# Block-sparse attention with the sampled blocks gathered on chip and the MLP woven in by half sequences

## The chip, the cores and the metric

The kernel runs on one core of one Trainium2 chip. The metric is the device time of one execution in microseconds (us), so smaller is better. A comparison is repeated in rounds on one chip, the kernel before next to the changed one.

Engines are called PE (TensorE, matrix products), PEld (its weight loads), ACT (ScalarE), DVE (VectorE), POOL (GpSimd) and SP (SyncE, here an issuer of DMAs). The traces list the instructions of each apart, as its queue; what the order of such a queue can cost is measured below for DVE (9.6 and 23.1 us of waiting in front of two copies).

## The reference, cut to what matters

```python
batch, n_heads, seq, head_dim = 4, 8, 768, 64
block, n_blocks, n_rand = 32, 24, 3
scores = (q @ k.T) / sqrt(64)
mask = |blk_i - blk_j| <= 1  or  blk_i in (0, 23)  or  blk_j in (0, 23)
for qb in range(24):
    for kb in sampled_blocks[qb]:        # 3 random key blocks, known only at run time
        mask[qb's rows, kb's columns] = True
x = softmax(where(mask, scores, -1e9)) @ v      # reshaped to 3072 x 512
out = gelu(x @ w_in) @ w_out                    # w_in 512 x 2048, w_out 2048 x 512
```

A query block in the middle sees its own key block and two neighbours, the first and the last block, and three sampled ones, so at most 8 blocks of 24. The first and the last query block see all 24. The inputs are float32, the kernels compute in bf16. q and k are drawn at 0.1 times a normal deviate, so all scores are close to zero.

## The kernel before: the parts that the change and the argument touch

```python
# attention, two heads at a time; all 24 x 24 blocks are computed, masked ones too.
# The mask is added inside the product: 64 extra rows of q (one-hot) and k (mask row).
for gi, (b, h) in enumerate(grp):
    for t in range(NT):                                   # 6 tiles of 128 keys
        sp = spsum_pool.tile([P, S], F32, tag="sp")
        for c0 in range(0, S, 512): nc.tensor.matmul(sp[:, c0:c1], ...)
        ex = exps_pool.tile([P, S], BF16, tag="ex")
        nc.scalar.activation(ex, sp, AF.Exp, scale=scale)          # L168: 128 x 768
# ... 6 x 6 products with V for each head, division, and then:
        nc.sync.dma_start(out=x_dram[...], in_=ao)                 # x goes to DRAM, 192 DMAs

# only after all attention: weights, and x back from DRAM, transposed
nc.gpsimd.dma_start(out=w_in_sb, in_=...); nc.gpsimd.dma_start(out=w_out_sb, in_=...)
for ki in range(KIN):
    nc.sync.dma_start(out=xT[:, ki, :], in_=x_dram[:, ki*P:(ki+1)*P], transpose=True)
# ... MLP in 6 tiles of 512 tokens: matmul hp (L214), Gelu (L218), matmul op (L220)
```

The softmax here doesn't subtract the row's maximum and nothing guards it: scores larger than these inputs give would overflow.

## Time and profile before

The kernel before took 463.65 us (median of 4 runs, 461.46 to 466.43) in the measurement beside the change.

| stretch, us | what happens | PE busy |
|---|---|---|
| 0 to 23 | set-up, mask | 0.42 |
| 23 to 243 | attention, no MLP | 179.5 of 220 |
| 243 to 292 | hole: weights and x are fetched | 4.88 of 49 |
| 292 to 467 | MLP, no attention | 166.04 of 175 |

The table comes from the windows view of the kernel before (a profiled execution with a span of 467.0 us). Its columns are: window and length in us, then busy us (and count of instructions) of PE, PEld, DVE, ACT and POOL, the granted PE clock as a fraction of full speed, the busy share of the DMA engines, GB/s.

```profile
0.00:23.00 23.00, 0.42 (x3) 0.26 (x4) 2.40 (x16) 1.28 (x1) 7.56 (x23) 1.00 0.37 32
23.00:145.00 122.00, 99.62 (x1038) 61.60 (x1037) 70.04 (x429) 78.19 (x104) 49.23 (x75) 0.94 1.12 94
145.00:243.00 98.00, 79.85 (x887) 49.60 (x883) 55.03 (x339) 66.07 (x89) 28.72 (x46) 0.93 0.84 73
243.00:292.00 49.00, 4.88 (x11) 1.46 (x12) 0.00 (x0) 0.96 (x1) 1.90 (x2) 0.51 1.13 150
292.00:467.00 175.00, 166.04 (x741) 66.64 (x756) 0.00 (x0) 69.78 (x121) 0.00 (x0) 0.99 0.10 37
```

The reader should see three stages with different limits. In the fourth line PE all but stands still (4.88 us busy of 49) and its granted clock is 0.51 on average, against 0.93 in the line before and 0.99 in the one after.

The groups view of the kernel before names the two costs that the change aims at. After the bar stand busy us and mean ns of one, then the idle time of the engine just before these instructions and what ended it.

```profile
L168 ACT ACTIVATE ex<-sp 128x768 bf16<-128x768 f32 x192 | 144.3, 808 | 92.0 <-PE op L176 56.7
L214 PE MATMUL hp<-xT,w_in_sb 128*128 128x512 bf16 x375 | 96.1, 384 | 45.8 <-DMA w_in_sb<-in_moe_w_in_dram 29.4
```

And the DMA view of the same kernel shows why the hole is there (the last number is us from issue to landing):

```profile
w_in_sb<-in_moe_w_in_dram POOLq DMA_DIRECT2D x1, 2048.0 KB, 26.2
w_out_sb<-in_moe_w_out_dram POOLq DMA_DIRECT2D x1, 2048.0 KB, 38.8
xT<-x_dram SPq DMA_TRANSPOSE x4, 28.4
```

The 192 dense exps fill 144 us of ACT, and the first MLP products wait 29.4 us for weights that are asked for only when the attention is over.

### The profile page before, as it was taken

Reading aid. Unit: us, or ns where it says so; the run is one execution under the profiler, and the core shown is the slowest. Engines: PE = TensorE matmul, PEld = TensorE weight load, DVE = VectorE, ACT = ScalarE, POOL = GpSimd, SP = SyncE. Lnnn points to the kernel's source line nnn. Section 1 sums busy time; section 2 is a strip of 40 time slices with the busy share of each in tenths; the row PEclk is TensorE's granted clock in tenths of the full one; section 3 lists DMA queues with packets and bytes.
Section 4 is the critical chain, followed back from the end, with each engine's and each line's share of the span. In section 5 each row is a group of like instructions: output and inputs, shape, how many; then the busy total and the mean of one; then the engine's idle time right before and its main releaser. Section 6 shows DMA issues by size and latency. Waiting matters only on the chain.

```text
span 467.0 us, 7913 instructions
## 1 busy us (share of the span) xinstructions
PE 350.8 (75%) x2672; PEld 179.6 (38%) x2688; DVE 127.5 (27%) x783; ACT 216.3 (46%) x314; POOL 87.4 (19%) x145
## 2 busy tenths in 40 slices
PE   0087878787788788889740003999999999999994
PEld 0054545554455455555420001333433443443341
DVE  1055756554556465566430000000000000000000
ACT  1055767667567676777720000335344353433533
POOL 1453434324334333441000000000000000000000
PEclk9999999888999898899975555999999999999999
DMA  0799999799899799997219999002011020200202
GB/s 1 68 133 99 96 101 98 70 91 84 73 100 97 70 98 96 100 80 60 27 22 156 131 176 162 1 0 91 0 41 51 0 91 0 84 7 0 92 0 90
DMA packets 174200, 33.11 MB, mean 71 GB/s; under 512 B 168528, under 2 KB 170576, under 8 KB 174160
## 3 DMA queue, kind: packets, MB, share of 16 engines
q0 software_dynamic: 77856, 13.64, 38.1%
q1 hardware_dynamic: 96304, 18.98, 25.8%
q8 instruction: 21, 0.34, 0.3%
q14 instruction: 19, 0.16, 0.1%
HBM read 27.34 MB, written 9.44 MB: 79 GB/s over the span
## 4 chain that ended last, share of the span: by engine, by line
PE 54%; DMA 15%; ACT 12%; SPq 9%; issue 5%; DVE 3%; POOL 0%; DVEq 0%; ACTq 0%; POOLq 0%
PE op L220 18%; PE hp L214 17%; ACT ex L168 11%; PE sp L165 10%; DMA x_dram<-ao 9%; SPq L198 9%; PE op L176 6%; DMA sb_i_80<-in_sampled_blocks_dram 2%; PE pt L151 1%; DMA xT<-x_dram 1%; DVE ao L182 1%; DMA q_sb<-in_q_dram 1%; DMA k_sb<-in_k_dram 1%; DVE kT L155 1%; DVE recip L180 1%
## 5 line engine op out<-in xcount | busy, mean ns | idle before, releaser
L168 ACT ACTIVATE ex<-sp 128x768 bf16<-128x768 f32 x192 | 144.3, 808 | 92.0 <-PE op L176 56.7
L214 PE MATMUL hp<-xT,w_in_sb 128*128 128x512 bf16 x375 | 96.1, 384 | 45.8 <-DMA w_in_sb<-in_moe_w_in_dram 29.4
L165 PE MATMUL sp<-qT,kT 128*128 128x512 bf16 (+1 forms) x384 | 103.9, 352 | 8.8 <-ACT ex L168 3.2
L218 ACT ACTIVATE g<-hp 128x512 bf16<-128x512 f32 x96 | 57.1, 597 | 98.8 <-PE hp L214 98.3
L220 PE MATMUL op<-w_out_sb,g 128*128 128x512 bf16 x377 | 94.9, 380 | 3.2 <-ACT g L218 2.5
L176 PE MATMUL op<-v_sb,ex 128*128 128x65 bf16 x1152 | 80.2, 199 | 22.6 <-DVE ao L182 13.0
L176 PEld LDWEIGHTS <-ex 128*128 128x128 bf16 x1152 | 62.6, 101 | 66.5 <-DVE ao L182 27.1
L214 PEld LDWEIGHTS <-w_in_sb 128*128 128x128 bf16 x384 | 37.8, 99 | 93.5 <-issue 50.7
L151 PE MATMUL pt<-identity,q_sb 128*128 128x128 bf16 x192 | 44.1, 230 | 26.3 <-DMA q_sb<-onehot_sb 21.7
L182 DVE TENSOR_SCALAR ao<-op,recip 128x64 bf16<-128x64 f32 x192 | 49.4, 279 | 22.5 <-DMA x_dram<-ao 21.9
L152 DVE COPY qT<-pt 128x128 bf16<-128x128 bf16 x192 | 41.3, 215 | 45.4 <-PE sp L165 23.8
L220 PEld LDWEIGHTS <-g 128*128 128x128 bf16 x384 | 30.3, 97 | 58.1 <-ACT g L218 33.8
L165 PEld LDWEIGHTS <-kT 128*128 128x128 bf16 x384 | 34.7, 103 | 18.3 <-issue 15.6
L180 DVE RECIPROCAL recip<-op 128x1 f32<-128x1 f32 x192 | 28.8, 164 | 25.8 <-PE op L176 17.1
L151 PEld LDWEIGHTS <-q_sb 128*128 128x128 bf16 x192 | 19.6, 102 | 34.8 <-issue 27.6
L133 POOL DMA_DIRECT2D q_sb<-in_q_dram x32 | 26.7, 834 | 20.7 <-DVE maskrow_sb L100 5.6
L140 POOL DMA_DIRECT2D v_sb<-in_v_dram x32 | 26.5, 828 | 6.6 <-POOL v_sb L139 6.5
L135 POOL DMA_DIRECT2D k_sb<-in_k_dram x32 | 27.0, 843 | 0.6 <-PE pt_822 L154 0.5
L218 ACT ACT_TABLE_LOAD x1 | 1.3, 1283 | 52.7 <-PE hp L214 52.7
L139 POOL MEMSET v_sb<- 128x6 bf16 x32 | 4.1, 129 | 102.2 <-PE pt L151 86.3
L154 PEld LDWEIGHTS <-k_sb 128*128 128x128 bf16 x192 | 19.5, 102 | 9.8 <-issue 7.6
L225 ACT COPY os<-op 128x512 f32<-128x512 f32 x24 | 12.9, 596 | 3.1 <-DMA out_dram<-os 2.6
(413 smaller groups left out, 94.0 us busy)
## 6 DMA issues: line engine op xcount, KB each, us to landing
out_dram<-os SPq DMA_DIRECT2D x24, 256.0 KB, 2.1
q_sb<-onehot_sb SPq DMA_DIRECT2D x32, 96.0 KB, 3.1
q_sb<-in_q_dram POOLq DMA_DIRECT2D x32, 96.0 KB, 3.8
k_sb<-maskrow_sb SPq DMA_DIRECT2D x32, 96.0 KB, 4.0
k_sb<-in_k_dram POOLq DMA_DIRECT2D x32, 96.0 KB, 4.1
v_sb<-in_v_dram POOLq DMA_DIRECT2D x32, 96.0 KB, 3.7
x_dram<-ao SPq DMA_DIRECT2D x192, 16.0 KB, 2.0
w_in_sb<-in_moe_w_in_dram POOLq DMA_DIRECT2D x1, 2048.0 KB, 26.2
```

The source lines that it names most:

```text
L135: nc.gpsimd.dma_start(out=k_sb[:, :, :D], in_=k[b, h].rearrange("(t p) d -> p t d", p=P))
L151: nc.tensor.transpose(pt, q_sbs[gi][:, t, :], identity)
L152: nc.vector.tensor_copy(qT[:, t * P:(t + 1) * P], pt)
L165: nc.tensor.matmul(sp[:, c0:c1], lhsT=kTs[gi][:, t * P:(t + 1) * P], rhs=qTs[gi][:, c0:c1], start=True, stop=True)
L168: nc.scalar.activation(ex, sp, AF.Exp, scale=scale)
L176: nc.tensor.matmul(op, lhsT=exps[gi][t][:, m * P:(m + 1) * P], rhs=v1_sbs[gi][:, t, :], start=(t == 0), stop=(t == NT - 1))
L180: nc.vector.reciprocal(recip, op[:, D:D + 1])
L182: nc.vector.tensor_scalar_mul(ao, op[:, 0:D], recip)
L198: nc.sync.dma_start(out=xT[:, ki, :], in_=x_dram[:, ki * P:(ki + 1) * P], transpose=True)
L214: nc.tensor.matmul(hp, lhsT=w_in_sb[:, ki, m * P:(m + 1) * P], rhs=xT[:, ki, n * NTILE:(n + 1) * NTILE], start=(ki == 0), stop=(ki == KIN ...
L218: nc.scalar.activation(g, hp, AF.Gelu)
L220: nc.tensor.matmul(op_tiles[ti], lhsT=g[:, ti * P:(ti + 1) * P], rhs=w_out_sb[:, m, :], start=(m == 0), stop=(m == KOUT - 1))
```

## The change

The intent is fourfold. Only the visible blocks are computed. The sampled blocks are gathered at run time: K inside SBUF by an indirect copy on POOL, V from a scratch tensor in DRAM by an indirect DMA, which POOL also issues. x stays on chip. And the MLP of one half sequence (384 tokens) is woven together with the attention of the next: the hidden layer of half h with the preparation of the next batch, the output layer of half h with the attention of half h+1. The weights load early.

```diff
-    mask24_dram = dram.tile([NB, NB], F32)
-    x_dram = dram.tile([N_TOK, D_MODEL], BF16)
... (dense attention, DMA transposes and separate MLP removed)
+    def prep_v(b, v_st, st):
+        pj = v_pj[0]
+        nc.vector.tensor_copy(
+            pj[:, :, :, 0:D], v_st.rearrange("p h (j d) -> p j h d", d=D))
... (to DRAM, and back in natural order)
+    def gather_v(b, hb, st):
...
+        for i in range(NQH):                                   # 11 query blocks of a half
+            qi = hb * NQH + i
+            nc.gpsimd.indirect_dma_start(
+                out=vg[:, i, :], out_offset=None, in_=v_dram[b][:, :],
+                in_offset=bass.IndirectOffsetOnAxis(ap=idx_v[:, qi:qi + 1], axis=0))
...
+    def gather_k(b, hb, hp, st):                               # one of 4 head pairs
...
+        nc.gpsimd.indirect_copy(dv[:, 0:32, :], kv, idx_k[:, hb, 0:2], i_know_this_is_slow=True)
+        nc.gpsimd.indirect_copy(dv[:, 32:44, :], kv, idx_k[:, hb, 2:3], i_know_this_is_slow=True)
...
+    for half in range(2 * B):
...
+            if hb == 0:
+                for w in "kqv":
+                    load(b + 1, w)                             # issued by POOL (casts to bf16)
+                vst = stage["v"]
+                fill.append(lambda nst=nst, b=b, vst=vst: prep_v(b + 1, vst, nst))
+            for hp in (2 * hb, 2 * hb + 1):
... (transposes of K and Q of the next batch)
+                fill.append(lambda hp=hp, nst=nst, b=b: gather_k(b + 1, 0, hp, nst))
+            if hb == 1:
+                fill.append(lambda nst=nst, b=b: gather_v(b + 1, 0, nst))
+        merge(hidden_steps(b, hb, st), fill)
+
+        if half + 1 < 2 * B:
+            merge(attention_steps(nb_, nhb, sts[nb_]), output_steps(b, hb, st))
+            if nhb == 0:
+                for hp in range(NPAIR):
+                    gather_k(nb_, 1, hp, sts[nb_])
+                gather_v(nb_, 1, sts[nb_])
```

A static scheduler moves instructions within each engine's queue before anything runs.

## The prediction

> **What bounds the kernel now.** Busy time by stretch (the windows view) shows a sequence. 0-23 us: set-up, PE busy 0.4 us. 23-243 us: attention, with no MLP work; PE busy 82% (179 us of 220), ACT 66%. 243-292 us: a hole, PE busy 4.9 us, clock 0.51: the weights are loaded only now (26 us and 39 us from issue to landing) while the DMA transposes bring x back from DRAM (28 us median). 292-467 us: MLP, PE busy 166 of 175 us; the chain of waits is almost all matmuls, 8 in 1.73-1.79 us (0.22 us each for 512 columns).
>
> **Removed.** (a) The 49 us hole: weights load early, x stays on chip. (b) 192 DMA writes of x and 64 DMA fills of mask columns. (c) Dense scores: 192 exps of 128x768 at 808 ns, 144 us of ACT; 384 wide score matmuls (104 us PE busy) and 1152 PV matmuls. (d) The strict order attention then MLP.
>
> **Added, by estimate from durations in the trace.**
> PE: the MLP stays, 384 output matmuls x 0.22 plus 512 hidden ones of 384 columns x 0.165 = 169 us. Attention becomes about 1984 + 384 small matmuls; six 65-column matmuls with their loads now take 0.36 us including 0.2 us latency, so some 30 ns each: 74 us[...] and 304 transposes x 56 ns = 17 us. PE floor about 275 us.
> ACT: exps (1024+704+128 columns x 32, 768 x 16) about 78 us, Gelus 64 x 0.8 = 52 us, plus 16 table loads at 1.28 us, since Exp and Gelu now alternate by half. About 150 us; not the limit.
> DVE: PSUM copies[...], masks, normalisation: about 130 us.
> POOL: the new risk. 32 K gathers of 44 indices. [...]V: 88 indirect DMAs at 1.0-1.3 us (plain ones took 0.83 us), about 100 us. POOL total 270-330 us: about as long as PE.
>
> **Critical path.** Prologue: sampled blocks land at 10 us (as now), then index arithmetic on DVE, first K gather near 13-15 us; V goes through DRAM and back; the gathers of half 0 run serially on POOL before the w_in loads are issued. First MLP matmul about 50-60 us, with PE mostly idle. Then eight halves of hidden + (output merged with next attention): PE floor per half 21 us MLP + about 12-13 us attention, with stalls 36 us. 55 + 8 x 36 = 343 us.
>
> **Prediction.** 345 us, 8 in 10 between 300 and 415. Faster by over 2%: 0.93; within 2%: 0.03; slower: 0.04.
>
> **What would show each step.** No hole with PE idle and clock near 0.5 after the prologue; ACT exp time about halved; small matmuls issued some 30 ns apart; MLP about 170 us of PE; table loads about 16; POOL busy above 70% of the span; in the chain, PE first and POOL gathers second, the gathers above all in the prologue and in second halves of each batch, whose K and V gathers are queued only just before.
>
> **What would make it wrong.** K gathers over 9 us each: POOL alone then needs over 400 us and bounds the kernel. [...] Short PE waits lowering the clock. In the other direction, gathers of 2-3 us and a prologue of 35 us would give under 310 us.

What no trace of the kernel before supports is cut from this text, terms of sums among it. The PE terms that are left come to 260 us (169 + 74 + 17); the sum, 275 us, holds a cut allowance, and so do the 12 to 13 us of attention for a half (the terms left give 11.4 us). Of POOL's total of 270 to 330 us the V gathers are about 100 us; most of the rest stood for the K gathers, an estimate that no trace supported. As for the terms that are left: a single 65-column matmul was recorded at 199 ns on average (L176, x1152), which is the 0.2 us of latency, and the 0.165 us and 56 ns are estimates, the 0.22 us of 512 columns (8 in 1.79 us) scaled to 384 and 128. For the clock, the profile before shows 0.93 to 0.94 during the attention, where PE is busy for 82% of the time, and 0.99 in the MLP, where it is busy for 95%.

## The result, and the profile after

The changed kernel took 430.6 us (median of 4 runs, 427.82 to 431.70) against 463.65 us. The ratio is 0.927, with a 95% interval of 0.921 to 0.934. All ratios in this document are taken from the fast runs of the same rounds, so they are not quite the ratio of the medians quoted. The change is faster, as predicted, but the time is 86 us above the predicted 345 us and outside the range of 300 to 415 us.

The groups view after, to be held against the one of before:

```profile
L286 POOL INDIRECT_COPY kg<-tk,idx_k 128x1024 bf16 x32 | 56.4, 1763 | 112.5 <-issue 44.0
L441 ACT ACTIVATE g<-hp 128x768 bf16<-128x768 f32 x64 | 51.5, 811 | 170.6 <-PE hp L439 76.3
...
L287 POOL INDIRECT_COPY kg<-tk,idx_k 128x384 bf16 x32 | 36.9, 1154 | 14.6 <-issue 13.3
...
L256 POOL DMA_INDIRECT vg<-v_dram_189,idx_v x22 | 21.2, 963 | 12.9 <-PE og L354 6.7
```

The exps of 144 us are gone; ACT as a whole fell from 216.3 to 142.9 us (the page's list of busy times). A K gather is the pair of lines L286 and L287, a V gather is L256. But PE, with 288.6 us of work in a span of 429.1 us, is busy for only 67% of it. The windows view after, in slices of 20 us, shows where it stands still:

```profile
80.00:100.00 20.00, 4.80 (x60) 2.30 (x57) 1.31 (x3) 2.27 (x5) 14.52 (x15) 0.50 0.41 90
...
120.00:140.00 20.00, 10.97 (x82) 5.81 (x82) 4.03 (x8) 0.00 (x0) 14.77 (x15) 0.74 0.93 234
...
180.00:200.00 20.00, 3.77 (x82) 2.23 (x83) 0.00 (x0) 3.83 (x5) 13.46 (x12) 0.67 0.34 71
...
340.00:360.00 20.00, 19.24 (x267) 12.18 (x267) 8.04 (x16) 14.34 (x19) 8.72 (x6) 1.00 0.04 15
```

The last line is what the prediction had in mind (19.2 of 20 us). The first three are not. All the slices in which PE is busy for less than 12 of 20 us lie in the first 160 us or between 180 and 200 us, that is in the first half of the run. The starts of the hidden layers of the eight halves, read from the timeline of the hidden-layer matmuls, say the same: 64.3, 137.4, 212.9, 250.0, 299.5, 338.6, 374.7 and 404.3 us. The prologue is 64 us (55 predicted). The six halves from 212.9 us on take 216 us, the predicted 36 each on average. That agreement is chance: their starts lie 29.6 to 49.5 us apart, and on another chip the same six took 197.5 us (below). The first two take 73.1 and 75.5 us, together 77 us more than 2 x 36. So in this sum the whole miss sits in the prologue (9 us) and in these two halves (77 us).

The waits view after gives suspects (in all, how often, longest, in us):

```profile
ACT g L441 <- remote: 61.6, 6, 30.8
...
DVE v_pj L235 <- DMA st_v<-in_v_dram: 37.4, 3, 23.0
...
PE og L354 <- DMA vg<-v_dram_186,idx_v: 20.2, 17, 4.7
PE od L376 <- DVE xd L344: 20.1, 1, 20.1
```

L235 is the copy of a new batch's V on DVE. The timeline of DVE shows it at work (start, length, what; in brackets the idle time before it and what ended that):

```profile
118.82 0.73 DVE L264 COPY pm<-st_k 128x768 bf16<-128x768 bf16 x1
129.15 0.96 DVE L235 COPY v_pj<-st_v 128x3072 bf16<-128x3072 bf16 x1 [9.61 <-DMA st_v<-in_v_dram]
...
179.04 0.56 DVE L344 TENSOR_TENSOR x<-og,rc 128x384 bf16<-128x384 f32 x1
202.65 0.96 DVE L235 COPY v_pj<-st_v 128x3072 bf16<-128x3072 bf16 x1 [23.05 <-DMA st_v<-in_v_dram]
```

At 118.82 us DVE ends a copy. The next instruction in its queue is the copy of V for a later batch, whose data have only been asked for at 118.45 us. DVE waits 9.6 us, later 23.1 us, with ready work behind it: after 179.04 us the normalisation of finished attention (L343, L344) stood in the queue, and PE waited for that in turn (20.1 us, L376). DVE did not take that work past the waiting copy: it did nothing at all in the window from 180 to 200 us (0.00 us busy), and L343 and L344 follow at 203.52 and 203.71 us, behind the copy at 202.65 us. The scheduler had moved these copies ahead: among DVE's working instructions the two stand at places 118 and 148, while in the kernel that keeps them in program order (x1_prepv_pinned, below) they stand at 166 and 238.

The timeline of POOL shows why the load was not there:

```profile
72.76 1.65 POOL L286 INDIRECT_COPY kg<-tk,idx_k 128x1024 bf16 x1 [2.00 <-issue]
74.82 1.11 POOL L287 INDIRECT_COPY kg<-tk,idx_k 128x384 bf16 x1 [0.41 <-issue]
77.94 1.99 POOL L286 INDIRECT_COPY kg<-tk,idx_k 128x1024 bf16 x1 [2.00 <-issue]
80.74 1.11 POOL L287 INDIRECT_COPY kg<-tk,idx_k 128x384 bf16 x1 [0.82 <-issue]
82.03 1.06 POOL L256 DMA_INDIRECT vg<-v_dram_186,idx_v  x1 [0.18 <-issue]
83.39 0.99 POOL L256 DMA_INDIRECT vg<-v_dram_186,idx_v  x1 [0.30 <-issue]
...
94.76 0.96 POOL L256 DMA_INDIRECT vg<-v_dram_186,idx_v  x1 [0.30 <-issue]
95.72 0.97 POOL L89 DMA_DIRECT2D st_k<-in_k_dram  x1
96.67 0.93 POOL L89 DMA_DIRECT2D st_q<-in_q_dram  x1
97.56 0.92 POOL L89 DMA_DIRECT2D st_v<-in_v_dram  x1
```

Four K gathers, each a pair of instructions, then eleven V gathers, then, at 95.72 us, the issue of the loads for the next batch. POOL takes these one after the other from 20.9 us on. The loads cast float32 to bf16, and this kernel issues them all on POOL, so they queue behind gathers that have nothing to do with them. One K gather takes 5.18 us from start to start (72.76 to 77.94): 1.65 and 1.11 us recorded, and 2.00 and 0.41 us before them in which POOL waits for nothing that the profile shows. The 2.00 us belong to the gather: none of the 32 has less before it, and before the V gather that follows one at 82.03 us they are missing. One V gather takes 1.26 us from start to start. So the gathers of one half cost POOL 4 x 5.18 + 11 x 1.26 = 34.6 us, and of all eight 277 us.

### The profile page after: what moved, and what is told of

The parts are those of the page before. It is cut to its first block, busy times and chain, and to the rows that moved or that the text cites. A ratio compares the mean times of both kernels' runs of the same rounds, so it can differ in the third digit from the quotient of the medians.

```text
span 429.1 us, 8099 instructions
## 1 busy us (share of the span) xinstructions
PE 288.6 (67%) x3532; PEld 174.0 (41%) x3568; DVE 148.2 (35%) x327; ACT 142.9 (33%) x192; POOL 206.7 (48%) x212
## 5 line engine op out<-in xcount | busy, mean ns | idle before, releaser
L439 PE MATMUL hp<-xT,w_in_sb 128*128 128x384 bf16 x512 | 94.4, 341 | 27.9 <-ACT g L441 17.5
L286 POOL INDIRECT_COPY kg<-tk,idx_k 128x1024 bf16 x32 | 56.4, 1763 | 112.5 <-issue 44.0
L441 ACT ACTIVATE g<-hp 128x768 bf16<-128x768 f32 x64 | 51.5, 811 | 170.6 <-PE hp L439 76.3
L354 PEld LDWEIGHTS <-pt 128*32 128x32 bf16 (+1 forms) x992 | 28.7, 103 | 37.8 <-issue 24.3
L287 POOL INDIRECT_COPY kg<-tk,idx_k 128x384 bf16 x32 | 36.9, 1154 | 14.6 <-issue 13.3
L306 DVE TENSOR_TENSOR pt<-pt,mask_x 128x768 bf16<-128x768 bf16 x32 | 22.9, 723 | 61.0 <-ACT pt L305 58.6
L268 PE MATMUL ps<-ident,pm 128*128 128x128 bf16 x192 | 19.0, 256 | 24.6 <-DVE ident L110 15.9
L354 PE MATMUL og<-vg,pt 128*32 128x65 bf16 x704 | 18.9, 207 | 20.6 <-DMA vg<-v_dram_186,idx_v 20.2
L459 DVE COPY os<-op 128x512 f32<-128x512 f32 x24 | 16.6, 690 | 33.2 <-PE op L455 26.2
L256 POOL DMA_INDIRECT vg<-v_dram_189,idx_v x22 | 21.2, 963 | 12.9 <-PE og L354 6.7
L256 POOL DMA_INDIRECT vg<-v_dram_188,idx_v x22 | 21.4, 973 | 12.4 <-PE og L354 6.4
L256 POOL DMA_INDIRECT vg<-v_dram_187,idx_v x22 | 21.8, 989 | 7.4 <-issue 6.4
L376 PE MATMUL od<-v_nat,pd 128*64 128x65 bf16 x192 | 11.1, 215 | 20.1 <-DVE xd L344 20.1
L256 POOL DMA_INDIRECT vg<-v_dram_186,idx_v x22 | 21.3, 968 | 6.5 <-issue 6.5
L343 DVE RECIPROCAL rc<-og 128x6 f32<-128x6 f32 x32 | 6.1, 192 | 46.8 <-PE og L354 46.7
L376 PEld LDWEIGHTS <-pd 128*64 128x64 bf16 x192 | 9.1, 127 | 23.5 <-issue 22.6
```

The costliest lines, as they stand in the source:

```text
L256: nc.gpsimd.indirect_dma_start(out=vg[:, i, :], out_offset=None, in_=v_dram[b][:, :], in_offset=bass.IndirectOffsetOnAxis(ap=idx_v[:, qi:q ...
L268: nc.tensor.transpose(ps[:, j, :], pm[:, j, :, :].rearrange("p h d -> p (h d)"), ident)
L286: nc.gpsimd.indirect_copy(dv[:, 0:32, :], kv, idx_k[:, hb, 0:2], i_know_this_is_slow=True)
L287: nc.gpsimd.indirect_copy(dv[:, 32:44, :], kv, idx_k[:, hb, 2:3], i_know_this_is_slow=True)
L306: nc.vector.tensor_tensor(pt[:, 0, :, 0:HALF], pt[:, 0, :, 0:HALF], mask_x[:, hb * MH:hb * MH + MH, :].rearrange("p m c -> p (m c)") .unsq ...
L354: nc.tensor.matmul(o, lhsT=l, rhs=r, start=first, stop=True, skip_group_check=True)
```

## The experiments

The texts number the theories. Theory 1: the queue order, that is the V copy at the head of DVE's queue waiting for a late load. Theory 2: the V gathers, that is their indirect DMAs. A third, called POOL's throughput later, the time of the gathers on POOL as such, came out of the first batch. Later texts call "theory A" the order of the instructions and "theory B" the chip.

| run (label) | chip | what | median us | ratio to before |
|---|---|---|---|---|
| first measurement | not recorded | changed kernel | 430.6 | 0.927 |
| a0_after_again | 0 | changed kernel | 430.6 | 0.928 |
| c0_after_third | 12 | changed kernel | 409.1 | 0.887 |
| d0_after_fourth | 9 | changed kernel | 408.6 | 0.875 |
| x1_prepv_pinned | 9 | V copies pinned | 382.4 | 0.826 |
| c1_pin_again | 12 | the same | 380.9 | 0.826 |
| d1_pin_third | 9 | the same | 382.0 | 0.818 |
| e1_pin_fourth | 12 | the same | 381.9 | 0.817 |
| x2_loads_first | 0 | loads early | 427.5 | none given |
| x8_pin_loads | 0 | pinned and loads early | 427.4 | none given |
| c8_pin_loads_again | 12 | the same | 377.8 | 0.819 |
| x3_v_plain_pool | 9 | V: plain copies on POOL | 376.7 | 0.813 |
| x4_v_none | 9 | no V gather | 355.4 | 0.769 |
| x5_v_plain_sp | 12 | V: plain copies on SP | 354.2 | 0.767 |
| x6_k_none | 9 | no K gather | 349.9 | 0.755 |
| d4_pin_loads_v_sp | 9 | order repaired, V on SP | 337.4 | 0.724 |
| d5_pin_loads_k_none | 9 | order repaired, no K gather | 323.3 | 0.692 |
| x7_kv_none | 0 | no gather at all | 310.9 | 0.669 |
| e7_kv_none_again | 12 | the same | 313.6 | 0.669 |

All runs had three rounds. The verdict for the runs on chip 12 of the c batch and x5 is formally "unclear", because three runs of the kernel before in that batch were over 1.5% above its fastest and were set aside; the ratios use the other four, and the differences are far above 2%. The two runs without a ratio spread so widely (421.65 to 431.42 and 420.41 to 429.89 us) that two runs of x2 and three of x8, the profiled one of x8 among them, counted as slow, being over 1.5% above the fastest; the fast ones took 421.65 and 423.59 us (x2) and 420.41 us (x8). One K gather instruction for all 44 blocks, in place of the pair, does not compile, and one indirect DMA with 11 indices in each partition is rejected when the program is built.

### V copies pinned to their place (x1_prepv_pinned)

```diff
-        nc.vector.tensor_copy(
+        copied = nc.vector.tensor_copy(
             pj[:, :, :, 0:D], v_st.rearrange("p h (j d) -> p j h d", d=D))
+        if b:
+            tc.keep_in_program_order(copied)
```

Nothing is removed, the scheduler just may not move these three copies ahead. The result is correct.

> Only VectorE's copy of V (st_v to v_pj) is pinned behind the VectorE work that the program states before it, from the second batch on; right result. Theory 1 (VectorE runs in order and stands for 10 and 23 us behind a V copy that was ordered a batch too early, whose load is queued behind gathers on POOL): these two waits vanish, 395 to 415 us. Rival (POOL's own throughput sets the pace, the waits only move): 425 to 435 us, within 2% of the changed kernel's 430.6.

It took 382.4 us (381.83 to 383.34), better than even theory 1 had hoped. Why it overshot became clear only with the c batch: the chip was another one. On the same chip, pinning is worth 409.1 - 380.9 = 28 us (chip 12), and 408.6 - 382.0 = 27 us (chip 9). In the changed kernel on chip 12, DVE stood 42.1 us in all before the V copies; with the pin 4.2 us are left. In the timeline of DVE of c1_pin_again the place where the changed kernel stopped at 118.82 us now reads:

```profile
118.31 0.34 DVE L266 COPY pm<-st_k 128x768 bf16<-128x768 bf16 x1
120.39 0.20 DVE L345 RECIPROCAL rc<-og 128x6 f32<-128x6 f32 x1 [1.73 <-PE og L356]
120.62 0.56 DVE L346 TENSOR_TENSOR x<-og,rc 128x384 bf16<-128x384 f32 x1
```

DVE goes on with the normalisation. Theory 1 is shown: two copies too early in DVE's queue cost about 28 us (the pin also holds a third, which had not waited). The pinned kernel computes and moves the same as the changed one.

### V gathers as plain copies, or none; no K gather (x3_v_plain_pool, x4_v_none, x6_k_none)

All three make the data wrong and leave the rest of the program alone. In x3 the address is fixed, so that POOL issues a plain DMA of the same size:

```diff
-            nc.gpsimd.indirect_dma_start(
-                out=vg[:, i, :], out_offset=None, in_=v_dram[b][:, :],
-                in_offset=bass.IndirectOffsetOnAxis(ap=idx_v[:, qi:qi + 1], axis=0))
+            nc.gpsimd.dma_start(out=vg[:, i, :], in_=v_dram[b][BLOCK * qi:BLOCK * qi + P, :])
```

In x4 and x6 the gathered tile is a constant, filled once:

```diff
-        for i in range(NQH): ... nc.gpsimd.indirect_dma_start(out=vg[:, i, :], ...)
+        st["vg", hb] = vg_fixed                # x4: memset to 0.5 at the start
...
-        nc.gpsimd.indirect_copy(...)           # both pieces
+        st["kg", hb, hp] = kg_fixed            # x6: memset to 0.01 at the start
```

> Each of the 88 indirect V gathers becomes a plain DMA of the same 128 rows x 1040 B from the same queue (fixed rows, wrong result on purpose); the order of instructions is otherwise nearly the same. Theory 2 (while an indirect gather runs, TensorE is slowed: a hidden group of 8 matmuls took 4.3 or 7.1 us instead of 1.3): groups are back at 1.3 us although the copies run, 385 to 410 us. Rival (the bytes landing in SBUF slow it, not their being indirect): groups stay at 4 to 7 us, 415 to 432 us.

> No V gathers: the weighted sums read one constant tile (wrong result on purpose). POOL loses 88 x 1.26 = 111 us. Theories 1 and 2 together (late loads, slowed TensorE) both lose their cause: 340 to 365 us. Rival (K gathers on POOL, 5.2 us each with the gap before them, are the limit): over 385 us.

> No K gathers: scores read one constant tile (wrong result on purpose). POOL loses 32 x 5.2 = 166 us, V gathers stay. If POOL's throughput is the cause: 340 to 360 us. If theories 1 and 2 are: V gathers still slow TensorE, but loads come earlier: 375 to 400 us.

They took 376.7, 355.4 and 349.9 us. Against 408.6 us of the changed kernel on the same chip (measured there later), plain copies save 32 us, no V gather 53 us, no K gather 59 us. In x3 the copies cost POOL 552 ns each and no 0.3 us between them, in place of 1.26 us, and DVE still stands 37 us before its V copies. So it is not the bytes and not the queue order alone. Time taken off POOL shortens the run, but by a third to a half of what it took there: 32 of 62 us in x3 (88 x 0.71), 53 of 111 us in x4, 59 of 166 us in x6. x6 contradicts the view that theories 1 and 2 are everything (they said 375 to 400 us): K gathers, which issue no DMA at all, cost at least as much as the V gathers. But these runs do not separate POOL's time from the order, because everything that is taken off POOL also makes its loads earlier.

x3 and x4 gave wrong results (relative errors 0.71 and 49.8). x6 passed the comparison with the reference although its K was a constant. With scores this close to zero the comparison can't see the content of the sampled K blocks at all, which is worth knowing before one trusts it for a K gather.

### The loads early, alone and with the pin; no gather at all (a0_after_again, x2_loads_first, x8_pin_loads, x7_kv_none)

x7 is the edits of x4 and x6 together. The early loads are:

```diff
             if hb == 0:
-                for w in "kqv":
-                    load(b + 1, w)
                 vst = stage["v"]
 ...
+        if hb == 1 and b + 2 < B:
+            for w in "kqv":
+                load(b + 2, w)
```

and the same for batch 1 ahead of the gathers of half 1. Unaltered, the changed kernel ran beside them.

> The changed kernel unaltered, a second look, in the same batch as the next three. Expected by every theory: 427 to 433 us. It also tells apart two readings of the first profile, in which groups of hidden-layer matmuls signalled their end 2 to 4 us after their recorded end: if that belongs to this order of instructions, the late signals come again at about the same places (near 137, 213, 250 and 300 us); if it was an accident of that one execution, they are gone while the time stays.

> Only the loads of K, Q and V of the next batch are traced before the gathers of a second half, so that POOL issues them about 35 us earlier; the copies of V stay where the static order put them. Theory 1 (the hoisted copy of V heads VectorE's queue and waits for its load, issued late on POOL): the copy still heads the queue but its load is there, the 9.6 and 23.1 us waits of VectorE shrink below 5 us, and the time is 385 to 410 us, like the pinned copy (382). Rival, that the place of the copy in VectorE's queue alone matters and not the time of the load: under 3% gain, 418 to 431 us.

> Both corrections: the copies of V keep their program place and the loads come before the gathers. Theory 1 with theory 2 (the K and Q copies for the next batch also wait for loads behind the gathers, which is what is left of the idle stretches at 80 to 115 and 142 to 158 us of the pinned kernel): 355 to 375 us. Rival, that what is left is the gathers' own time on POOL and not the loads' place: 378 to 386 us, no better than the pinned copy alone.

> Wrong on purpose: no gather at all, constant tiles in their place, all else kept. POOL does only setup and loads. Expected if POOL's gathers (time and queue) are the whole excess over the predicted 345 us: 310 to 335 us, near 275 us of TensorE work plus a prologue of 40 to 50 us. If over 345 us, something other than the gathers (load bandwidth, weights, clock) costs as well.

They took 430.6, 427.5, 427.4 and 310.9 us. Two of the expectations failed badly: by the medians the kernel with both repairs was hardly better than the changed kernel, and 45 us worse than the pin alone in the first batch (by its one fast run, 420.41 us, it was 10 us better and 38 us worse). In x2 the first of the two waits of DVE was gone, but the second was still 25.2 us and not below 5. Taken at face value, "early loads undo the pin". The trace said otherwise. In a0, x2 and x8, as in the first measurement, groups of matmuls reported their end late. If PE's ends and its semaphore's records are paired in order, then 28 to 33 times in each run (some records are missing, so the count is not exact) the signal of a matmul came more than 0.4 us after its recorded end, in a0 by up to 12.6 us, while in the x1, x3, x4 and x6 runs this happened 0 or 1 times (0.65 us). The timeline of ACT in a0 shows the effect in one hidden layer:

```profile
147.24 0.81 ACT L441 ACTIVATE g<-hp 128x768 bf16<-128x768 f32 x1 [34.02 <-remote]
150.78 1.51 ACT L441 ACTIVATE g<-hp 128x768 bf16<-128x768 f32 x2 [2.74 <-remote]
```

PE's records place the eight products for the first of these Gelus between 135.44 and 136.91 us; the Gelu starts at 147.24 us, right when PE's semaphore moves (147.21 us). So the recorded end of a matmul and its signal can part, by 10.3 us here (136.91 to 147.21 us).

Also, completion records of DMAs were missing. In the batch on chip 9 the traces hold 16 of them for nearly every V gather; in a0, x2 and x8 there were 16 for the loads that landed before the first V gather (at 34 us), and from then on 4 to 5 on average for a gather (the texts say 4). The waits for these gathers did end, so it is the records that are missing. With so few left the profile could not say when the gathers landed. The first measurement is of the same kind (about 30 late signals; counted from one issue on a semaphore to the next, 16 records for 20 of POOL's 22 loads and 5.6 on average for a V gather).

All three kernels with the ailment had run on chip 0, those without it on chip 9. That left two readings: the order of the instructions, or the chip.

### The order or the chip (c1_pin_again, c0_after_third, c8_pin_loads_again, x5_v_plain_sp)

Three kernels were run again without an edit, in one batch, on whatever chip came: it was chip 12. In the fourth, V is copied plainly by SP's queue:

```diff
-            nc.gpsimd.indirect_dma_start(
-                out=vg[:, i, :], out_offset=None, in_=v_dram[b][:, :],
-                in_offset=bass.IndirectOffsetOnAxis(ap=idx_v[:, qi:qi + 1], axis=0))
+            nc.sync.dma_start(out=vg[:, i, :], in_=v_dram[b][BLOCK * qi:BLOCK * qi + P, :])
```

> The kernel with pinned V copies once more, now beside the unaltered changed kernel. The first batch (382 us here, no late semaphore signals, 16 completion records for each V gather) and the second (428 to 431 us for three other orders, late signals, 4 records for each gather) ran on different chips. Theory A, the order of instructions decides: 382 us again on whatever chip. Theory B, the chip decides (on one of them the completion signals of indirect DMAs come slowly and hold up TensorE's signals): this kernel takes 410 us or more if this chip is of that kind, 382 if not, and always moves with the next run.

> The unaltered changed kernel on the same chip. Theory A: 427 to 433 us, with late signals. Theory B: either about 430 us together with a pinned kernel over 410 us, or 390 to 405 us together with a pinned kernel at 382 us.

> Pinned copies and early loads, on the same chip. Theory A: 420 to 430 us as before. Theory B on a chip without slow signals: 350 to 375 us; on a chip with them: 420 to 430.

> Wrong on purpose: the 88 V gathers are plain copies of the same rows' bytes issued on SP's hardware queue, so that POOL has the K gathers alone and no indirect DMA runs. Theory of POOL's queue: like the kernel with no V gather (355 us) within 10 us, on either kind of chip, with no late signals. Rival, that the bytes of the V rows (11.7 MB) cost as such: over 370 us.

They took 380.9, 409.1, 377.8 and 354.2 us. Theory A is refuted: the very same changed kernel takes 409.1 us here and 430.6 us on chip 0, and the same kernel with both repairs 377.8 us here and 427.4 us there (420.4 us in its one fast run). Theory B's own numbers were missed by a little: it had said 390 to 405 us for the changed kernel and 350 to 375 us with both repairs. And what theory 2 set out from, matmuls that slow down while an indirect gather runs, is not seen here: all 88 V gathers run in c0, c1 and c8, and no matmul's signal is over 0.4 us late, apart from records after the last matmul. The DMA view of a0_after_again (chip 0) has no landing time for the V gathers,

```profile
vg<-v_dram,idx_v POOLq DMA_INDIRECT x88
```

and that of c0_after_third (chip 12) has one, 2.8 us:

```profile
vg<-v_dram,idx_v POOLq DMA_INDIRECT x88, 2.8
```

On the eight semaphores that the V gathers use (some loads share them), a0 left 811 records, c0 1764. And the Gelus of the hidden layer that stalled in a0 follow each other at 1.3 to 2 us in c0:

```profile
136.92 0.81 ACT L441 ACTIVATE g<-hp 128x768 bf16<-128x768 f32 x1 [23.39 <-PE hp L439]
138.22 0.81 ACT L441 ACTIVATE g<-hp 128x768 bf16<-128x768 f32 x1 [0.49 <-PE hp L439]
140.19 0.81 ACT L441 ACTIVATE g<-hp 128x768 bf16<-128x768 f32 x1 [1.16 <-PE hp L439]
```

So on chip 0, in that batch, signals came slowly once indirect DMAs ran. It took both, as far as these runs go: x7, with no V gather, ran on chip 0 with no late signal and 310.9 us. What exactly is slow on that chip, and whether it is the chip or its condition in those minutes, is open. Each execution here was recorded by the profiler, so it is also open whether the signals would be slow without it. Nor is it a lower clock: the runs of a0 agree within 1%, and d0 below is 20 us faster in its profile at a lower granted clock (0.857 against 0.876).

x5 confirms that the bytes of the V rows are not the cost: moved by another queue they cost nothing against no V gather at all (354.2 on chip 12 against 355.4 us on chip 9).

### With the order repaired: is it POOL's throughput? (d4_pin_loads_v_sp, d5_pin_loads_k_none, d1_pin_third, d0_after_fourth)

With pin and early loads, 378 us is left on a chip with prompt signals, still 33 us above the prediction. The groups view of c8_pin_loads_again, POOL alone, shows what POOL does (busy us and mean ns, then idle us before):

```profile
L258 POOL DMA_INDIRECT vg<-v_dram,idx_v x88 | 85.5, 972 | 26.2 <-issue 23.4 <-DMA st_v<-in_v_dram 0.6 <-PE og L356 0.6
L288 POOL INDIRECT_COPY kg<-tk,idx_k 128x1024 bf16 x32 | 54.4, 1701 | 80.0 <-issue 40.5 <-DVE pm L266 13.8 <-PE sd L333 7.2
L289 POOL INDIRECT_COPY kg<-tk,idx_k 128x384 bf16 x32 | 37.3, 1165 | 13.7 <-issue 12.8 <-PE sd L333 0.5 <-DVE tk L271 0.4
```

Adding start-to-start times as above, the gathers occupy 277 us and the loads 14 us. From its first gather at 20.4 us to the end of the last at 330.2 us POOL has 309.8 us, so beyond the usual gaps it was idle for 19 us only. The chain is simple: 20.4 us until the indices are there, 309.8 us of POOL, 45.8 us of work on PE that is left after the last gather, together 376.0 us, the span. That is an argument, not a proof. The test takes V off POOL in one run and K in the other, with both repairs in place (no new edit: d4 is the edits of x1, x2 and x5 together, d5 those of x1, x2 and x6; d1 and d0 are the pinned and the changed kernel as they were).

> Wrong on purpose: order repaired (pinned V copies, early loads) and the 88 V gathers replaced by plain copies on SP's queue, so that POOL has 20.7 us of K gathers in each half and not 34.6. Theory of POOL's throughput: POOL is now well under TensorE's 31 to 36 us for a half, every half from the second on takes 31 to 40 us, and the time is 315 to 340 us. Rival, that a wait's place is still at fault: over 345 us, near the 354 us of the same copies without the repair.

> K gathers replaced by a constant tile with the order repaired; POOL has 13.9 us of V gathers in each half. Theory of POOL's throughput: 310 to 335 us on a chip without slow signals (20 us more with them). Rival: over 340 us, near the 350 us of the same without the repair.

> The pinned kernel on whatever chip this is. If this chip has slow signals (4 completion records for a V gather): 400 us or more, as the unaltered kernel lost 21 us by them. If not: 380 to 383 us.

> The unaltered changed kernel on the same chip: 428 to 432 us with slow signals, 408 to 411 us without; anything between would mean that the two kinds of chip are not all there is.

They took 337.4, 323.3, 382.0 and 408.6 us, on chip 9. Both expected times held: about 40 us fall with V and 55 us with K, against the 377.8 us of c8. (c8 ran on chip 12 and was not repeated on chip 9; the pinned kernel took 380.9 and 382.0 us on the two.) Two halves of d4 took 40.7 and 40.5 us, just over the 31 to 40 us expected of each. In the pages' slices (40 equal parts of the span, tenths busy), c8_pin_loads_again has three holes in PE (slices 8 to 9, 14 to 16 and 24 to 25) while POOL is never free for long:

```profile
PE   0256238319799460797999960899999999999995
POOL 8556766557667866463576755451776655410000
```

In d4_pin_loads_v_sp POOL has pauses, and PE has none of those holes after the first quarter:

```profile
PE   0156481199999959999999599999999997999995
POOL 8736685463302555343004655133015543000000
```

And in d5_pin_loads_k_none:

```profile
PE   0068476299999559999999999999999999999995
POOL 8925793247677300047872000177710000000000
```

(POOL's digits count recorded time only; the 2.00 and 0.41 us inside each K gather look like idleness.) The starts of the hidden layers, read from the timelines, put it in numbers. All but the last column are on chips with prompt signals:

| interval, us | predicted | changed (c0) | repaired (c8) | repaired, V on SP (d4) | repaired, no K (d5) | no gather (x7, chip 0) |
|---|---|---|---|---|---|---|
| to the first hidden layer | 55 | 64.2 | 63.7 | 68.0 | 52.1 | 50.8 |
| half 0 | 36 | 71.2 | 50.6 | 32.1 | 40.3 | 37.2 |
| half 1 | 36 | 73.8 | 60.6 | 40.7 | 42.8 | 34.7 |
| halves 2 to 7 | 216 | 197.5 | 201.1 | 194.1 | 186.5 | 185.9 |

POOL needs 34.6 us of gathers and some 2 us of issues for a half, PE 31 to 35 us when undisturbed (the halves of x7). So POOL is the slower stage, it starts with no head start, and the first halves pay for it. In halves 2 to 7 of c8 only one interval is still long (49.7 us); while PE stood still, gathers had run ahead, and the last half has no attention after it.

### The floor on another chip, and the pin again (e7_kv_none_again, e1_pin_fourth)

Two kernels once more, without an edit.

> Wrong on purpose, no gather at all. With no V gather there is no indirect DMA whose completion could come slowly, so the kind of chip should not matter: 309 to 313 us on any chip. If it is over 316 or under 306 us, chips differ in more than the signals.

> The pinned kernel. On a chip without slow signals 380 to 383 us; on one with them over 395 us.

They took 313.6 us (310.87 to 314.96) and 381.9 us, on chip 12. The first is slightly above the expected 309 to 313 us, but its range covers what chip 0 showed, so the floor of 311 to 314 us does not hang on the chip. No batch met a chip with slow signals again, so how the pinned kernel does there is open.

## Why the prediction was right or wrong

**Right: what bounds the kernel before and what goes away.** The hole of 49 us is gone, ACT went to 142.9 us (predicted: about 150), the table loads are 16 of 1.28 us, the MLP and attention together give a PE floor that x7 confirms: 261.5 us busy in its page, and 311 us of time with everything but the gathers (predicted: PE floor about 275 us, which contains an allowance that no trace supported). Here is the busy line of that page:

```profile
PE 261.5 (85%) x3529; PEld 162.3 (53%) x3568; DVE 134.2 (43%) x327; ACT 142.4 (46%) x192; POOL 33.0 (11%) x62
```

**Right: the size of the V gathers, and POOL's total.** V was predicted at 1.0 to 1.3 us and took 1.26 us; POOL's total of 270 to 330 us was right too (277 us of gathers and 14 us of loads). The part of it that stood for the K gathers no trace supported; that it fitted is partly luck. A K gather took 5.18 us: 2.76 us recorded for 44 indices, which is 63 ns for one, and 2.41 us of gaps, so 118 ns for one from start to start. What fills the gaps the trace does not show.

**Slightly off: the prologue.** "First MLP matmul about 50-60 us"; it was 64 us, because the first gather started at 20.9 us and not at 13 to 15 us.

**Wrong: the sum "55 + 8 x 36 = 343 us".** It lets the eight halves follow each other at PE's pace. The halves from the third on kept that pace or bettered it (216 us for six in the first measurement, 197.5 us on chip 12), but the first two took 73.1 and 75.5 us (71.2 and 73.8 on chip 12). On chip 12 the account is 343 + 9 (prologue) + 73 (first two halves) - 18 (other six) = 407 us, the span. Three things stand in place of the missing term, and each was measured:

1. Queue order, about 31 us of the 64 us between 345 and 409 us. The prediction treated the halves as if every engine always worked on the oldest ready thing. Copies of V, placed early by the static scheduler, held DVE for up to 28 us each, and loads stood behind gathers on POOL. Pinning three copies gave 27 to 28 us back, moving the loads another 3 us (380.9 to 377.8 us on chip 12, ranges apart). How much the loads give without the pin is open: x2 was only measured on chip 0.
2. POOL as a pipeline stage, the other 33 us. The prediction had noted "about as long as PE" and then left POOL out of the sum. A stage of 291 us that can't start before 20 us and is followed by 46 us of other work can't give less than 357 us, even if it never pauses; the size of the stage was in the prediction, its place in the sum was not. d4 and d5 show it: relieve POOL of either gather and 40 or 55 us go. The split between this point and the first depends on which is taken first: with no gather, x7 reaches 311 us without any repair of the order, since the load that the V copy waits for then has no gather before it. V copies there wait 6.3 us at most. So of the 409 us, 95 to 98 us go with the gathers (x7 and e7), and 31 of them already with the order alone.
3. Slow signals on chip 0, and in the first measurement, whose chip is not recorded: 21 us for this kernel (430.6 against 409 us) and 43 us for the one with both repairs (its one fast run, 420.4, against 377.8 us; 50 us by the medians). This part is a comparison between chips; its cause is open. Nothing in the profile before could show this, since that kernel issues no indirect DMA; it runs alike on all chips (462.9 to 466.9 us). The recorded result lies outside the range because of it: 409 us would have been inside, but by luck, as the 64 us of points 1 and 2 were not in the sum.

**Of the listed risks, none was it.** K gathers over 9 us: the traces show none (5.18 us from start to start; the longest K gather piece took 3.12 us, against the usual 1.65 us). PE's clock did fall to 0.50 in the idle stretches (PE busy for 4.80 of 20 us), against the prediction's own sign ("No hole with PE idle and clock near 0.5 after the prologue"). But it came and went with them: it is 1.00 in the slice where PE is busy for 19.24 of 20 us, and in one batch on chip 0 the mean of the profiled run is 0.876 for the changed kernel (a0) and 0.994 without the gathers (x7). PE's busy time, 277.3 us in c0 and 261.5 us in x7, differs by 16 us.

The profile should have shown "POOL busy above 70% of the span". It shows 48%, and this is no evidence against POOL as the limit, since the gaps inside a K gather, 77 us in all (32 x 2.41), are not counted as busy.

Of the correct kernels, the one with the pin and early loads was the fastest on a chip with prompt signals, 377.8 us, 0.819 of the kernel before. The pin alone gives 380.9 to 382.4 us.

## What to carry to other kernels

When a change puts another engine into the pipeline, as POOL here with its gathers one after the other, write its lane into the sum: when it can start, how long it is from start to start (not by its busy time), and what has to follow it (here 20, 291 and 46 us). If that exceeds the lane of the main engine (277 us busy in c0), take it for the bound however idle it looks (48% busy in the first measurement), and test that by taking work off it. After a schedule has been made by a tool, look in each queue for an instruction that waits for a late load with ready work behind it; two such copies cost 28 us here and pinning them repaired it. And before two variants are compared, run both in one batch on one chip: two of our runs seemed to show that a repair undid another, when what had changed was the chip (or its condition at that time).
